# One order list for five engines: attention first, first-layer products in two large groups

## The chip, the cores and the metric

The kernel runs on one core of one Trainium2 chip. The metric is device microseconds (us) of one execution; lower is better. The engines are named as the profile names them: PE is TensorE's matrix multiplication and PEld its weight loads, DVE is VectorE, ACT is ScalarE, POOL is GpSimd, SP is SyncE, whose queue issues every DMA here.

## The reference

```
attn_out = attention(q, k, v)            # 2 batches x 12 heads, 448 tokens, head size 64, causal, float32
x = attn_out -> (896 tokens, 768)
h = x @ w_in                             # 768 -> 1024
solu = h * softmax(h);  ln = layernorm(solu) * g_ln
x = ln @ w_out                           # 1024 -> 768, the first block ends
h = max(x @ w_in2, 0);  out = (h * h) @ w_out2      # 768 -> 2048 -> 768, the second block
```

## The kernel before

Attention works on 12 pairs of heads (pair i of 0 to 11; pairs 0 to 5 are batch 0). Every float32 product after it is split: an operand is kept as a rounded part (hi) and a rest (lo), and three products replace one. The weights come as 64-bit floats, so DVE first puts a raw tile together with three integer operations (`as_f32`, lines 151 to 153).

Everything up to the second block is written as an order list, `SEQ`: names such as `Sa.7`, an operation and its index. A loop (line 732) hands the operations out in that order. Each engine runs its own operations in the order in which the list names them; between engines only data and buffers hold things back. So the list fixes five queues, and nothing else in the program depends on it. The names that matter here:

- SP: `load_r` (keys and queries of a pair into one of 4 `KQ` buffers, 448 KB), `load_v` (one of 3 `VR` buffers, 256 KB), `lq` (a quarter of a 1 MB weight tile of the first layer; `lq.8` to `lq.11` are tile 2), `ld` (a whole one, tiles 3 to 5), `rowd` (row maxima into `MR`, two small DMAs), `sums`, `rcd`, `spread` (denominators out, to DRAM, and back over all partitions), `lw` (weights of the second product), `load_g`.
- ACT: `H` (rounds `KQ`), `row`, `ea1` and `eb1` (exponentials of the scores), `E` (the unnormalised output out of PSUM), `x_hi`, `wh` (hi of a weight tile).
- DVE: `mxa`, `mxb`, `mxc` (row maxima), `recips`, `x_lo`, `wf` (`as_f32`), `wl` (lo of a weight tile), and `mx`, `mu` and others of the layernorm.
- POOL: `ka` and `kb` (causal mask), `ad` (adds for the row sums), `norm` (multiplies by the reciprocals, L421).
- PE: `fl` (filler products), `S0a`, `S0b`, `S0c` (rough scores for the maxima), `mT` (a transpose), `Sa` and `Sb` (scores), `Ua` and `Ub` (times v, L353), `Us` (row sums, L377), `h<t>.<c>` (first-layer products of token tile t with weight tile c, six matrix products, L497), `T` (transposes for the layernorm), `y0`, `y1` (second product).

PSUM is handed out in four slots of two banks. A slot is taken by `S0`, `S`, `U`, a token tile of `h`, `T` or `y`, and goes to the next taker in the order in which the list gives it back: by `mxa` and `mxb`, by `row`, by `ea1` and `eb1`, by `E`, and for an `h` tile by `sq`, its square in the layernorm:

```python
        def bank2(nm):
            pl = slots.pop(0)
...
            def h_part(b, t, c):
                for s, w in ((0, 0), (0, 1), (1, 0)):
                    for half in range(2):
                        nc.tensor.matmul(
                            b[:, half, :],
                            xT[c][s][:, t * P : t * P + P],
                            W1[c][:, w, 512 * half : 512 * half + 512],
```

So `h<t>.<c>` needs `x_hi` and `x_lo` of the head pairs of block c and of the batch of tile t, and `wh.<c>` and `wl.<c>`. Three token tiles (0 to 2) lie in batch 0 alone.

Of the kernel before, what the change touches and what calls it, by code (L numbers as in the profile page):

```python
# [27 lines left out]
SEQ = """
load_r.0 fl.0 fl.1 fl.2 H.0 fl.3 fl.4 S0c.0 fl.5 load_r.1 load_r.2 H.1 mxc.0 load_r.3 S0a.0 lq.0 fl.6 fl.7 S0b.0 S0a.1
fl.8 mxa.0 mxb.0 ld.3 S0b.1 mxr.0 H.2 mxa.1 mxb.1 Sa.0 load_v.0 S0c.1 H.3 S0b.2 S0b.3 mxc.1 ea1.0 mT.1 row.1 mxb.2  # L30
Sb.0 S0a.2 ka.0 lq.4 S0c.2 mxb.3 rowd.1 lq.1 eb1.0 mxa.2 load_r.4 lq.2 Sa.1 S0a.3 ea1.1 Ua.0 mxc.2 mT.2 kb.0 Sb.1
row.2 S0c.3 mxa.3 H.4 Ub.0 load_g.0 ad.0 eb1.1 mxc.3 ka.1 load_v.1 S0b.4 mT.3 rowd.2 Us.0 row.3 S0a.4 mxb.4 E.0
load_r.5 Sa.2 kb.1 S0c.4 Sb.2 mxa.4 lq.3 ea1.2 sums.0 load_v.2 mxc.4 eb1.2 Ua.1 rowd.3 ad.1 mT.4 recips.0 Sb.3 Ub.1
wf.0 Us.1 row.4 ka.2 H.5 lq.8 kb.2 eb1.3 rcd.0 S0a.5 Sa.3 E.1 load_r.6 ea1.3 ad.2 S0b.5 rowd.4 spread.0 ka.3 Sa.4
S0c.5 H.6 sums.1 mxa.5 mxb.5 lq.5 Sb.4 load_r.7 kb.3 S0a.6 recips.1 mxc.5 rcd.1 load_v.3 ea1.4 mT.5 norm.0 row.5 eb1.4
Ua.2 S0b.6 Ub.2 lq.6 H.7 S0c.6 mxa.6 mxb.6 spread.1 ka.4 Us.2 x_hi.0 rowd.5 Ua.3 S0a.7 mxc.6 E.2 ad.3 mT.6 lq.7 sums.2
x_lo.0 kb.4 load_r.8 S0b.7 load_v.4 wh.0 Ub.3 mxa.7 row.6 rowd.6 norm.1 Us.3 mxb.7 recips.2 S0c.7 Sb.5 E.3 x_hi.1 H.8
Sa.5 mxc.7 sums.3 mT.7 row.7 eb1.5 Sa.6 rcd.2 wf.1 recips.3 ad.4 ea1.5 x_lo.1 S0b.8 kb.5 ea1.6 load_r.9 spread.2 Sb.6
Ua.4 Ub.4 S0c.8 eb1.6 rowd.7 ka.5 mxb.8 H.9 norm.2 load_r.10 ad.5 S0a.8 mxa.8 rcd.3 Us.4 Sa.7 load_v.5 S0b.9 mxc.8 E.4
ea1.7 sums.4 Sb.7 mxb.9 S0a.9 mT.8 recips.4 kb.6 ka.7 Ua.5 spread.3 x_hi.2 row.8 S0c.9 Ub.5 H.10 load_r.11 rcd.4 mxa.9  # L40
mxc.9 x_lo.2 S0a.10 mT.9 eb1.7 rowd.8 ka.6 norm.3 Us.5 S0b.10 ad.6 row.9 lq.9 wh.1 mxa.10 Sa.8 Sb.8 load_v.6 E.5 H.11
mxb.10 rowd.9 load_v.7 S0c.10 wl.0 ea1.8 Ua.6 Ub.6 mxc.10 sums.5 kb.7 spread.4 S0b.11 x_hi.3 mT.10 recips.5 eb1.8
lq.10 row.10 Us.6 rcd.5 load_v.8 S0a.11 x_lo.3 norm.4 mxb.11 lq.11 rowd.10 Sa.9 ad.7 Ua.7 load_v.9 spread.5 mxa.11
wl.1 E.6 Ub.7 S0c.11 ka.8 Sb.9 ea1.9 mxc.11 x_hi.4 Sb.10 eb1.9 mT.11 Us.7 x_lo.4 h0.0 eb1.10 sums.6 wf.2 row.11 h1.0
norm.5 Sa.10 E.7 rowd.11 recips.6 wf.3 h1.1 ld.4 rcd.6 Ua.8 kb.8 ea1.10 Ub.8 ka.10 load_v.10 h0.1 wh.2 wl.2 h1.2 wh.3
Sb.11 ad.8 wl.3 h0.2 x_hi.5 h0.3 ld.5 load_v.11 spread.6 sums.7 h1.3 Us.8 eb1.11 x_lo.5 wf.4 norm.6 wh.4 E.8 ka.9 h2.0
recips.7 h2.2 wf.5 kb.9 h2.3 wl.4 Sa.11 rcd.7 wh.5 sums.8 x_hi.6 spread.7 recips.8 h2.1 wl.5 h0.4 lw.0 x_lo.6 h0.5
ea1.11 ad.9 Ua.9 Ub.9 rcd.8 mx.0 Us.9 norm.7 ka.11 h1.4 kb.10 of.0 E.9 h1.5 x_hi.7 mx.1 lw.1 ex.0 sums.9 ex.1 h2.4
Ua.10 h2.5 ad.10 Ub.10 recips.9 mu.0 mu.1 sq.0 h5.0 sq.1 Us.10 x_lo.7 spread.8 h5.1 de.1 norm.8 rcd.9 h3.0 x_hi.8 lw.2
kb.11 E.10 mx.2 x_lo.8 ex.2 Ua.11 ad.11 va.1 pw.1 h3.1 Ub.11 spread.9 de.0 norm.9 va.0 Us.11 sums.10 de.2 h5.2 oh.0  # L50
recips.10 x_hi.9 E.11 mu.2 rcd.10 pw.0 ol.0 fa.1 h4.0 sq.2 h4.2 spread.10 of.1 x_lo.9 sums.11 recips.11 va.2 ln.1
rcd.11 oh.1 fa.0 of.2 norm.10 spread.11 lw.3 h3.2 ln.0 h3.3 T.0 h5.3 x_hi.10 x_lo.10 h3.4 oh.2 pw.2 h4.3 ol.1 fa.2
h4.4 Th.0 Tl.0 T.1 ol.2 norm.11 x_hi.11 ln.2 x_lo.11 h3.5 Th.1 of.3 mx.3 h4.1 oh.3 h4.5 h5.4 Tl.1 T.2 ex.3 mu.3 de.3
h5.5 lw.4 sq.3 mx.4 h6.0 Th.2 va.3 pw.3 ex.4 mx.5 fa.3 h6.3 Tl.2 ln.3 mu.4 h6.1 T.3 ex.5 mu.5 de.4 Th.3 h6.4 sq.5 Tl.3
h6.2 sq.4 of.4 ol.3 lw.5 h6.5 oh.4 va.4 pw.4 mx.6 of.5 y0.0 ol.4 ex.6 de.5 mu.6 va.5 fa.4 oh.5 sq.6 de.6 y0.1 ln.4
lw.6 y0.2 va.6 pw.6 y0.3 l2.1 ol.5 pw.5 T.4 of.6 fa.5 oh.6 y0.4 Th.4 lw.7 fa.6 ln.5 y0.5 ln.6 ol.6 Tl.4 of.7 T.5 Th.5
oh.7 Tl.5 l2.0 l2.2 ol.7 y0.6 T.6 Th.6 Tl.6 f2.0 y0.7 y1.0 yo.0 y1.1 g2.0 yp.0 yo.2 o2.0 yo.1 f2.1 yp.1 g2.1 o2.1 y1.2
yp.2
"""


# [794 lines left out]
```

## Time and profile before

| what | value |
|---|---|
| median of 3 runs | 445.75 us (445.51 to 446.55) |
| the profiled execution | 445.59 us |
| its span, first to last instruction | 443.9 us |
| PE busy | 435.9 us (98%) |
| DVE busy | 268.6 us (61%) |
| ACT busy | 162.8 us (37%) |
| POOL busy | 151.9 us (34%) |
| second block starts | 209.30 us |

The span is 1.7 us shorter than the profiled execution's own time. Places in the text are microseconds from the start of the span. Busy time of PE counts a product until its last result is out, so it counts short waits between pipelined products too.

### The profile page before, as it was taken

The page shows a single profiled execution, that of the slowest core. Times are in us where ns is not written, and L with a number is a line of the kernel's source. Part 1 is how long each engine was busy: PE and PEld are TensorE (multiplying, and loading weights), DVE is VectorE, ACT ScalarE, POOL GpSimd, SP SyncE. Part 2 cuts the span into 40 slices and gives each one's busy share as a digit, 9 for nine tenths or more (in the row PEclk, how much of TensorE's full clock was granted, in tenths as well). Part 3 has the DMA queues.
Part 4 walks back from the last instruction along what each step waited for, and adds up shares of the span by engine and source line. Part 5 has one row for each costly group of instructions (what it writes and reads, how often), then busy time and mean ns, then how long its engine had stood idle before and what let it go on. Part 6 is the DMA issues. An engine that isn't in the chain of part 4 may idle for free.

```text
span 443.9 us, 6457 instructions
## 1 busy us (share of the span) xinstructions
PE 435.9 (98%) x2487; PEld 372.0 (84%) x2487; DVE 268.6 (61%) x511; ACT 162.8 (37%) x223; POOL 151.9 (34%) x145
## 2 busy tenths in 40 slices
...
GB/s 252 201 180 212 156 209 158 144 165 99 38 235 17 326 14 1 0 0 1 71 84 130 102 113 123 91 142 73 142 71 143 76 138 88 251 109 103 127 16 124
DMA packets 33000, 52.45 MB, mean 118 GB/s; under 512 B 5962, under 2 KB 24394, under 8 KB 32586
## 3 DMA queue, kind: packets, MB, share of 16 engines
...
## 4 chain that ended last, share of the span: by engine, by line
PE 92%; DMA 3%; POOL 2%; ACT 1%; SPq 0%; issue 0%; DVE 0%; POOLq 0%; ACTq 0%
PE h L780 26%; PE o L780 26%; PE h L497 14%; PE y L645 13%; PE s L309 4%; PE U L353 4%; DMA KQ<-in_kq_dram 2%; PE mxp L251 1%; PE T L623 1%; PE U L377 1%; DMA VR<-in_v_dram 1%; PE s L320 1%; PE s L328 1%; POOL x L421 1%; PE fill L526 0%; ACT HI L241 0%
## 5 line engine op out<-in xcount | busy, mean ns | idle before, releaser
L701 POOL TENSOR_TENSOR w<-wf,w 128x768 fp32r<-128x768 f32 x32 | 59.1, 1847 | 209.0 <-ACT w L698 209.0
L780 PE MATMUL h<-yT,w 128*128 128x480 f32 x576 | 115.4, 362 | 0.0
L780 PE MATMUL o<-g,w 128*128 128x480 f32 x576 | 115.4, 362 | 0.0
L780 PEld LDWEIGHTS h<-yT,w 128*128 128x128 f32 x576 | 107.9, 187 | 7.4
L780 PEld LDWEIGHTS o<-g,w 128*128 128x128 f32 x576 | 107.9, 187 | 7.3
L151 DVE TENSOR_SCALAR wf<-raw 128x768 int32<-128x768 int32 (+1 forms) x46 | 28.3, 616 | 79.3 <-DMA raw<-in_moe_w_out_dram 55.3
L698 ACT CAST w<-wf 128x768 fp32r<-128x768 f32 x32 | 26.8, 836 | 134.9 <-DVE wf L153 116.0
L497 PE MATMUL h<-w,xT 128*128 128x512 f32 x252 | 61.8, 397 | 0.0
L645 PE MATMUL y<-lnT,w 128*128 128x384 f32 (+1 forms) x288 | 59.1, 365 | 0.0
L645 PEld LDWEIGHTS y<-lnT,w 128*128 128x128 f32 x288 | 51.9, 188 | 6.1
L497 PEld LDWEIGHTS h<-w,xT 128*128 128x128 f32 x252 | 46.1, 188 | 11.1 <-issue 1.6
L152 DVE SCALAR_TENSOR_TENSOR wf<-raw,wf 128x768 int32<-128x768 int32 (+1 forms) x46 | 49.0, 1064 | 1.6
L153 DVE SCALAR_TENSOR_TENSOR wf<-raw,wf 128x768 int32<-128x768 int32 (+1 forms) x46 | 46.1, 1002 | 1.6
L266 DVE CUSTOM_DVE_ANT_0 JK<-mxp,MK 112x336 bf16<-112x336 f32 (+2 forms) x96 | 39.3, 446 | 10.6 <-PE mxp L251 9.3
L341 POOL TENSOR_SCALAR_AFFINE_SELECT PP<-PP 128x256 f32<-128x256 f32 (+1 forms) x48 | 26.4, 579 | 17.8 <-ACT PP L344 17.8
L344 ACT ACTIVATE PP<-s 128x1024 f32<-128x1024 f32 x24 | 24.2, 1018 | 17.1 <-PE s L320 14.7
L309 PE MATMUL s<-KQ 64*128 64x448 f32 (+3 forms) x192 | 26.6, 396 | 0.4 <-ACT PP L344 0.4
L762 DVE TENSOR_TENSOR relu<-h,relu 128x896 f32<-128x896 f32 x16 | 17.5, 1092 | 14.6 <-ACT relu L761 14.6
L353 PE MATMUL U<-PP,VR 128*64 128x448 f32 (+3 forms) x192 | 25.0, 389 | 0.9 <-DMA VR<-in_v_dram 0.7
L367 POOL TENSOR_TENSOR ps<-ps,PP 128x384 f32<-128x384 f32 (+1 forms) x24 | 24.7, 1030 | 1.9
L309 PEld LDWEIGHTS s<-KQ 64*128 64x128 f32 x192 | 16.7, 186 | 8.7 <-issue 5.3
L353 PEld LDWEIGHTS U<-PP,VR 128*64 128x64 f32 x192 | 11.6, 136 | 13.4 <-issue 9.0
...
## 6 DMA issues: line engine op xcount, KB each, us to landing
...
```

The source lines that it names most:

```text
L151: nc.vector.tensor_scalar(xi, hw, 3, 0x3FFFFFFF, ALU.logical_shift_left, ALU.bitwise_and)
L152: nc.vector.scalar_tensor_tensor(xi, hw, -0x40000000, xi, ALU.bitwise_and, ALU.bitwise_or)
L153: nc.vector.scalar_tensor_tensor(xi, lw, 29, xi, ALU.logical_shift_right, ALU.bitwise_or)
L266: nc.vector.tensor_tensor_reduce(JK[t], b[0:JP, h, o : o + nk], MK[:, S - nk :], 1.0, NEG, ALU.add, ALU.max, mx[i][:, 4 * h + t : 4 * h + ...
L309: nc.tensor.matmul(s[:, h, o : o + nq], K[r, P * t : P * t + P], Q[r, q0 : q0 + nq], start=t == HALF[a][0][0], stop=False,)
L341: nc.gpsimd.affine_select(ap, ap, [[0, 2], [1, m]], ALU.is_ge, 0.0, base=0, channel_multiplier=-1)
L353: nc.tensor.matmul(UB[i][D * h : D * h + D, 0, q0:S], VR[i % 3][:, t, h, :], PP[(2 * i + a) % NPP][:, h, o : o + nq], start=t == 0, stop=t ...
L497: nc.tensor.matmul(b[:, half, :], xT[c][s][:, t * P : t * P + P], W1[c][:, w, 512 * half : 512 * half + 512], start=(c == 0 and s == 0 and ...
L645: nc.tensor.matmul(b[:, ci, 0:n], WO[fi][:, w, c * P : c * P + P], M["lnT"][a][s][:, fi, :], start=(fi == 0 and w == 0 and s == 0), stop=( ...
L698: nc.scalar.copy(W2[n][:, 0], w_f["2", n])
L701: nc.gpsimd.tensor_tensor(W2[n][:, 1], w_f["2", n], f(W2[n][:, 0]), ALU.subtract)
L780: nc.tensor.matmul(flat(b)[:, o : o + n], w[:, wp, c : c + P], ops[s][:, x : x + n], start=first and r == 0, stop=last and r == 2,)
```

## The change

Only `SEQ` is replaced. It holds the same 585 operations, in another order; from `T.0` on the two lists differ little. The parts that matter, cut (a line of "..." is left-out text):

```diff
-Sb.0 S0a.2 ka.0 lq.4 S0c.2 mxb.3 rowd.1 lq.1 eb1.0 mxa.2 load_r.4 lq.2 Sa.1 S0a.3 ea1.1 Ua.0 mxc.2 mT.2 kb.0 Sb.1
-row.2 S0c.3 mxa.3 H.4 Ub.0 load_g.0 ad.0 eb1.1 mxc.3 ka.1 load_v.1 S0b.4 mT.3 rowd.2 Us.0 row.3 S0a.4 mxb.4 E.0
...
-x_lo.0 kb.4 load_r.8 S0b.7 load_v.4 wh.0 Ub.3 mxa.7 row.6 rowd.6 norm.1 Us.3 mxb.7 recips.2 S0c.7 Sb.5 E.3 x_hi.1 H.8
-Sa.5 mxc.7 sums.3 mT.7 row.7 eb1.5 Sa.6 rcd.2 wf.1 recips.3 ad.4 ea1.5 x_lo.1 S0b.8 kb.5 ea1.6 load_r.9 spread.2 Sb.6
-Ua.4 Ub.4 S0c.8 eb1.6 rowd.7 ka.5 mxb.8 H.9 norm.2 load_r.10 ad.5 S0a.8 mxa.8 rcd.3 Us.4 Sa.7 load_v.5 S0b.9 mxc.8 E.4
-ea1.7 sums.4 Sb.7 mxb.9 S0a.9 mT.8 recips.4 kb.6 ka.7 Ua.5 spread.3 x_hi.2 row.8 S0c.9 Ub.5 H.10 load_r.11 rcd.4 mxa.9
-mxc.9 x_lo.2 S0a.10 mT.9 eb1.7 rowd.8 ka.6 norm.3 Us.5 S0b.10 ad.6 row.9 lq.9 wh.1 mxa.10 Sa.8 Sb.8 load_v.6 E.5 H.11
...
-lq.10 row.10 Us.6 rcd.5 load_v.8 S0a.11 x_lo.3 norm.4 mxb.11 lq.11 rowd.10 Sa.9 ad.7 Ua.7 load_v.9 spread.5 mxa.11
-wl.1 E.6 Ub.7 S0c.11 ka.8 Sb.9 ea1.9 mxc.11 x_hi.4 Sb.10 eb1.9 mT.11 Us.7 x_lo.4 h0.0 eb1.10 sums.6 wf.2 row.11 h1.0
-norm.5 Sa.10 E.7 rowd.11 recips.6 wf.3 h1.1 ld.4 rcd.6 Ua.8 kb.8 ea1.10 Ub.8 ka.10 load_v.10 h0.1 wh.2 wl.2 h1.2 wh.3
-Sb.11 ad.8 wl.3 h0.2 x_hi.5 h0.3 ld.5 load_v.11 spread.6 sums.7 h1.3 Us.8 eb1.11 x_lo.5 wf.4 norm.6 wh.4 E.8 ka.9 h2.0
-recips.7 h2.2 wf.5 kb.9 h2.3 wl.4 Sa.11 rcd.7 wh.5 sums.8 x_hi.6 spread.7 recips.8 h2.1 wl.5 h0.4 lw.0 x_lo.6 h0.5
-ea1.11 ad.9 Ua.9 Ub.9 rcd.8 mx.0 Us.9 norm.7 ka.11 h1.4 kb.10 of.0 E.9 h1.5 x_hi.7 mx.1 lw.1 ex.0 sums.9 ex.1 h2.4
-Ua.10 h2.5 ad.10 Ub.10 recips.9 mu.0 mu.1 sq.0 h5.0 sq.1 Us.10 x_lo.7 spread.8 h5.1 de.1 norm.8 rcd.9 h3.0 x_hi.8 lw.2
-kb.11 E.10 mx.2 x_lo.8 ex.2 Ua.11 ad.11 va.1 pw.1 h3.1 Ub.11 spread.9 de.0 norm.9 va.0 Us.11 sums.10 de.2 h5.2 oh.0
...
+mxb.2 lq.1 rowd.1 mxa.2 S0c.2 ka.0 S0b.3 Sa.1 load_r.4 load_v.1 eb1.0 kb.0 mxc.2 ad.0 mT.2 mxb.3 ea1.1 ka.1 lq.2 Sb.1
+row.2 S0a.3 S0c.3 Ua.0 load_v.2 rowd.2 H.4 Ub.0 load_r.5 mxa.3 eb1.1 mxc.3 lq.3 S0c.4 kb.1 S0a.4 ad.1 mT.3 Us.0 row.3
...
+lq.6 load_r.8 mxa.7 kb.4 S0c.7 rowd.6 S0b.7 recips.2 Us.3 Sb.5 rcd.2 lq.7 norm.1 wh.0 mxc.7 E.3 mxb.7 sums.3 x_hi.1
+Ua.4 eb1.5 ad.4 H.8 Sa.5 lq.9 ea1.5 mT.7 x_lo.1 row.7 Sb.6 spread.2 S0b.8 eb1.6 kb.5 Sa.6 S0a.8 recips.3 ea1.6
+load_r.9 Ub.4 wf.1 mxb.8 Us.4 S0c.8 mxa.8 H.9 norm.2 E.4 rowd.7 ka.5 mxc.8 rcd.3 Sa.7 S0a.9 load_v.5 Sb.7 ea1.7 mT.8
+ad.5 S0b.9 mxa.9 S0c.9 load_r.10 x_hi.2 row.8 Ua.5 kb.6 spread.3 x_lo.2 mxb.9 ka.6 norm.3 Ub.5 sums.4 load_v.6 ad.6
+load_g.0 rowd.8 Us.5 ka.7 wh.1 mxc.9 recips.4 wl.1 Sa.8 H.10 eb1.7 S0a.10 E.5 mT.9 kb.7 load_v.7 Sb.8 ea1.8 S0b.10
...
+S0c.11 rowd.10 mxc.11 Sb.9 ld.4 mT.11 ea1.9 Sa.10 row.11 eb1.9 wl.0 x_hi.4 Sb.10 sums.6 x_lo.4 rowd.11 Us.7 lq.11
+load_v.9 ea1.10 spread.5 Ua.8 eb1.10 Ub.8 kb.9 norm.5 Sb.11 Sa.11 recips.6 Us.8 wf.2 eb1.11 lw.0 wf.3 ea1.11 wh.2 E.7
+h1.0 x_hi.5 ld.5 wl.2 wh.3 h1.1 wl.3 rcd.6 ka.9 spread.6 ka.10 x_lo.5 wf.4 kb.11 norm.6 h0.0 ka.11 wh.4 h0.1 h2.0 h1.2
+kb.10 sums.7 recips.7 wf.5 rcd.7 E.8 load_v.10 h2.1 sums.8 h2.2 lw.1 h1.3 wl.4 ad.9 h0.2 h2.3 Ua.9 wh.5 x_hi.6 Ub.9
+h0.3 wl.5 x_lo.6 recips.8 h0.4 spread.7 h0.5 h1.4 lw.2 h1.5 mx.0 mx.1 ex.0 Us.9 norm.7 E.9 rcd.8 mu.0 h2.4 h2.5 Ua.10
+ex.1 sq.0 load_v.11 sums.9 Ub.10 Ua.11 x_hi.7 Ub.11 ad.10 de.0 mu.1 va.0 ad.11 spread.8 recips.9 de.1 Us.10 x_lo.7
+sq.1 norm.8 va.1 E.10 mx.2 of.0 rcd.9 sums.10 ex.2 x_hi.8 recips.10 Us.11 x_lo.8 spread.9 pw.0 fa.0 h4.0 h5.0 mu.2
...
```

Between `Us.7` and `T.0`, PE's list before has 12 stretches of `h` operations, with attention between them; the new list has 4, two of them of 11 and of 8 operations.

## Rows read from the trace of the kernel before

**Rows 1.** The page: the span, and each engine's busy us (share) and instructions.
```profile
span 443.9 us, 6457 instructions
PE 435.9 (98%) x2487; PEld 372.0 (84%) x2487; DVE 268.6 (61%) x511; ACT 162.8 (37%) x223; POOL 151.9 (34%) x145
```

**Rows 2.** Busy time by stretch: length; PE, PEld, DVE, ACT, POOL; granted clock, DMA.
```profile
10.00:70.00 60.00, 57.77 (x546) 37.59 (x546) 50.05 (x196) 40.17 (x61) 48.56 (x64) 1.00 0.65 193
70.00:209.30 139.30, 139.30 (x760) 112.92 (x757) 98.90 (x154) 61.17 (x89) 46.02 (x42) 1.00 0.27 92
```

**Rows 3.** Timeline of PE: start, us, instructions, idle time before it in brackets.
```profile
21.82 0.47 PE L251 MATMUL mxp<-HI 64*128 64x336 f32 x4 [0.52 <-ACT HI L241]
...
46.54 1.13 PE L309 MATMUL s<-KQ 64*128 64x320 f32 x8 [0.44 <-ACT PP L344]
...
61.22 1.63 PE L353 MATMUL U<-PP,VR 128*64 128x448 f32 x12 [0.74 <-DMA VR<-in_v_dram]
```

**Rows 4.** The chain that ended last, in order of time: start, us, what.
```profile
15.38 5.37 DMA KQ<-in_kq_dram
...
50.81 1.13 PE s L309 x8
51.94 0.28 PE s L320 x2
...
56.83 4.25 DMA VR<-in_v_dram
...
70.30 0.19 PE mxp L278
...
71.00 2.95 PE h L497 x12
...
75.36 1.57 PE h L497 x6
...
83.06 4.31 PE h L497 x18
87.37 0.51 PE U L377 x10
...
97.89 1.88 PE U L353 x16
...
104.60 1.02 PE U L353 x8
...
117.40 7.04 PE h L497 x30
```

**Rows 5.** Timeline of SP, DMAs issued: `lq.1`, `sums.2`, `sums.4`, and `ld.4` behind `rowd.11`.
```profile
14.89 0.39 SPq L481 DMA_DIRECT2D raw<-in_moe_w_in_dram  x1
...
39.53 0.60 SPq L394 DMA_DIRECT2D sc<-es  x1
...
51.42 0.62 SPq L394 DMA_DIRECT2D sc<-es  x1
...
72.75 0.40 SPq L126 DMA_DIRECT2D raw<-in_moe_w_in_dram  x1
```

**Rows 6.** Timeline of ACT: the first part of `E.3`, and `H.8`.
```profile
41.48 0.45 ACT L386 ACTIVATE es<-U,SE 97x224 f32<-97x224 f32 x1 [1.60 <-issue]
...
44.48 0.94 ACT L241 CAST HI<-KQ 128x896 fp32r<-128x896 f32 x1 [1.51 <-DMA KQ<-in_kq_dram]
```

**Rows 7.** Timeline of DVE: `recips.2`, start of `wf.1`, end of `mxb.8`; `wf.2`, `wl.5`.
```profile
42.29 0.20 DVE L400 RECIPROCAL sr<-sc 112x8 f32<-112x8 f32 x1 [0.47 <-DMA sc<-es]
...
43.12 0.89 DVE L151 TENSOR_SCALAR wf<-raw 128x1024 int32<-128x1024 int32 x1
...
49.24 0.07 DVE L266 DVE_READ_ACCUMULATOR2_ANT mx<- 112x1 f32 x1
...
69.43 0.89 DVE L151 TENSOR_SCALAR wf<-raw 128x1024 int32<-128x1024 int32 x1
...
92.79 1.91 DVE L492 TENSOR_TENSOR w<-wf,w 128x1024 fp32r<-128x1024 f32 x1
```

More of the change, by code (lines that the diff above doesn't have):

```diff
@@ L28 @@
 SEQ = """
-load_r.0 fl.0 fl.1 fl.2 H.0 fl.3 fl.4 S0c.0 fl.5 load_r.1 load_r.2 H.1 mxc.0 load_r.3 S0a.0 lq.0 fl.6 fl.7 S0b.0 S0a.1
-fl.8 mxa.0 mxb.0 ld.3 S0b.1 mxr.0 H.2 mxa.1 mxb.1 Sa.0 load_v.0 S0c.1 H.3 S0b.2 S0b.3 mxc.1 ea1.0 mT.1 row.1 mxb.2
-Sb.0 S0a.2 ka.0 lq.4 S0c.2 mxb.3 rowd.1 lq.1 eb1.0 mxa.2 load_r.4 lq.2 Sa.1 S0a.3 ea1.1 Ua.0 mxc.2 mT.2 kb.0 Sb.1
-row.2 S0c.3 mxa.3 H.4 Ub.0 load_g.0 ad.0 eb1.1 mxc.3 ka.1 load_v.1 S0b.4 mT.3 rowd.2 Us.0 row.3 S0a.4 mxb.4 E.0
-load_r.5 Sa.2 kb.1 S0c.4 Sb.2 mxa.4 lq.3 ea1.2 sums.0 load_v.2 mxc.4 eb1.2 Ua.1 rowd.3 ad.1 mT.4 recips.0 Sb.3 Ub.1
@@ L34 @@
-wf.0 Us.1 row.4 ka.2 H.5 lq.8 kb.2 eb1.3 rcd.0 S0a.5 Sa.3 E.1 load_r.6 ea1.3 ad.2 S0b.5 rowd.4 spread.0 ka.3 Sa.4
-S0c.5 H.6 sums.1 mxa.5 mxb.5 lq.5 Sb.4 load_r.7 kb.3 S0a.6 recips.1 mxc.5 rcd.1 load_v.3 ea1.4 mT.5 norm.0 row.5 eb1.4
-Ua.2 S0b.6 Ub.2 lq.6 H.7 S0c.6 mxa.6 mxb.6 spread.1 ka.4 Us.2 x_hi.0 rowd.5 Ua.3 S0a.7 mxc.6 E.2 ad.3 mT.6 lq.7 sums.2
-x_lo.0 kb.4 load_r.8 S0b.7 load_v.4 wh.0 Ub.3 mxa.7 row.6 rowd.6 norm.1 Us.3 mxb.7 recips.2 S0c.7 Sb.5 E.3 x_hi.1 H.8
-Sa.5 mxc.7 sums.3 mT.7 row.7 eb1.5 Sa.6 rcd.2 wf.1 recips.3 ad.4 ea1.5 x_lo.1 S0b.8 kb.5 ea1.6 load_r.9 spread.2 Sb.6
@@ L39 @@
-Ua.4 Ub.4 S0c.8 eb1.6 rowd.7 ka.5 mxb.8 H.9 norm.2 load_r.10 ad.5 S0a.8 mxa.8 rcd.3 Us.4 Sa.7 load_v.5 S0b.9 mxc.8 E.4
-ea1.7 sums.4 Sb.7 mxb.9 S0a.9 mT.8 recips.4 kb.6 ka.7 Ua.5 spread.3 x_hi.2 row.8 S0c.9 Ub.5 H.10 load_r.11 rcd.4 mxa.9
-mxc.9 x_lo.2 S0a.10 mT.9 eb1.7 rowd.8 ka.6 norm.3 Us.5 S0b.10 ad.6 row.9 lq.9 wh.1 mxa.10 Sa.8 Sb.8 load_v.6 E.5 H.11
-mxb.10 rowd.9 load_v.7 S0c.10 wl.0 ea1.8 Ua.6 Ub.6 mxc.10 sums.5 kb.7 spread.4 S0b.11 x_hi.3 mT.10 recips.5 eb1.8
-lq.10 row.10 Us.6 rcd.5 load_v.8 S0a.11 x_lo.3 norm.4 mxb.11 lq.11 rowd.10 Sa.9 ad.7 Ua.7 load_v.9 spread.5 mxa.11
```

24 lines of the change are left out of this document (16 added, 8 removed).

## The prediction

> **What bounds the kernel now.** I read the page first, then busy time by stretch, then PE's own timeline for its idle time, then the chain that ended last, and last the queues of SP, ACT and DVE at the few places that the new order touches. PE is busy 435.9 of 443.9 us [rows 1]; the change moves none of its 2487 products to another engine and takes none away, so it can gain or lose only in the gaps between them. From 70 to 209.30 us PE has no idle time at all, and from 10 to 70 it has 60.00 − 57.77 = 2.23 us [rows 2]. The granted clock is 1.00 in both stretches, the upper level (2.4 GHz), so there is nothing to be had from it. Three idle places of PE in the attention stretch add up to 0.52 + 0.44 + 0.74 = 1.70 us [rows 3]. What follows 209.30 us is the second block, whose operations are not in the list; it moves as a whole.
>
> So the sum has three kinds of terms: products that cost less because of their neighbours, the three old waits, and new waits.
>
> **Fewer stretches of h (−1.7).** The chain gives four lengths of a stretch of h operations: one takes 1.57 us, two 2.95, three 4.31, five 7.04 [rows 4]. That is a line: 1.365 us for each operation and 0.21 for each stretch (1.365 + 0.21 = 1.575; 5 × 1.365 + 0.21 = 7.04). The list before has 12 stretches between Us.7 and T.0, the new one 4. 8 × 0.21 = 1.7 us less. The bounds are 0 and 1.7, and I take the whole, since the four rows agree to 0.01.
>
> A rule of the skill speaks against this term. The Trainium skill, TensorE: Matmul & The Clock Gate, Back-to-back issue gap, gives an isolated spacing of N ÷ 2.4 plus 2.5 ns for a product of N columns, the drain of one hidden behind the next; worked out from it, six products of 512 columns are an estimated 1.29 us wherever they stand, and a stretch costs nothing extra. By it this term and the next would be 0. The rows of one, two, three and five show otherwise, so I keep 0.21.
>
> **U operations side by side (−0.5).** An Ua or Ub alone takes 1.02 us, a pair that follows each other 1.88 [rows 4], so 2 × 1.02 − 1.88 = 0.16 less. I count five adjacent pairs in the list before and ten in the new one, and Ub.10 there also meets Ua.11: six new joints, 6 × 0.16 = 0.96 at most. What used to stand between them makes joints elsewhere, which no row prices; I take the middle of 0 and 0.96.
>
> **The three old waits (−1.7).** (a) S0b.4 waited 0.52 us for H.4, and H.4 for load_r.4, issued at 15.38 behind lq.1 (14.89) and landed 5.37 later [rows 3 to 5]. In the new list load_r.4 follows rowd.1 directly and lq.1 has been gone long before; issued at 14.89 even the same 5.37 us end at 20.26, and with an H of 0.94 us [rows 6] PE, which reached this point at 21.82 − 0.52 = 21.30, finds it done. (b) Sb.6 waited 0.44 for the PSUM slot of eb1.5, which on ACT stood behind H.8, and H.8 had kept ACT idle 1.51 us for its load [rows 3, 6]. In the new list eb1.5 stands ahead of H.8. (c) Ua.6 waited 0.74 for load_v.6, issued at 56.83 and 4.25 us on its way [rows 3, 4], behind rowd.8, lq.9 and a load_r. In the new list load_v.6 follows sums.4, which is issued at 51.42 [rows 5]: some five us earlier. All three go. (At the ends, pipelined products hide 0.1 or 0.2 us more of each wait; 2.1 is the other end.)
>
> **New wait 1: Sa.7 (+0.3).** Sa.7 takes its PSUM slot from mxb.8, in both lists; PE got there at 50.81 [rows 4]. DVE had it done at 49.31 [rows 7]. In the new list recips.3 stands ahead of wf.1, so DVE must first wait for sums.3 to land. sums.3 can leave when the first part of E.3 is written: 41.48 + 0.45 = 41.93 [rows 6], less a lead of some 0.8 by then (0.52 and three joints), 41.1. A transfer of that kind was awaited from 39.53 to 42.29, 2.76 us [rows 5, 7]; so recips.3 runs at 43.9, and wf.1 begins there instead of at 43.12. From wf.1's start to mxb.8's end is 49.31 − 43.12 = 6.19 us [rows 7], less for recips.3 and x_lo.1, which now stand ahead: mxb.8 ends at 49.3 to 50.1. PE comes at 50.81 − 0.52 − 0.44 − 0.25 = 49.6, earlier if more than the idle time is saved. Between 0 and 1.1; I take 0.3.
>
> **New wait 2: the weights of the first large group (+1.0).** In the list before 14 h operations stand ahead of Ua.9, in 6 stretches, and Ua.9 starts at 97.89 [rows 4]; in the new one 11 in one stretch, and otherwise the same. PE gets there at 97.89 − 3 × 1.365 − 5 × 0.21 − 1.7 − 0.4 + 0.3 = 91.0, and to h0.4, which needs wl.4, after 1.88 for Ua.9 and Ub.9 and 1.4 for h0.3: at 94.3; to h0.5, which needs wl.5, at 95.7. DVE's row from the start of wf.2 to the end of wl.5 was 94.70 − 69.43 = 25.3 us [rows 7]. wf.2 needs lq.11, and in the new list lq.11 stands on SP behind rowd.11, which waits for row.11 and that for mT.11. The group starts at 91.0 − 11 × 1.365 − 0.21 = 75.8; between mT.11 and it stand four S operations of 1.13 + 0.28 at most, a pair of U of 1.88 and two Us of 0.51 [rows 4], 8.5 us, so mT.11 ends at 67.3. Before, it ended at 70.49, and the DMA behind rowd.11 was issued at 72.75 [rows 4, 5], 2.26 later; here 69.6. A quarter tile then takes between 2.76 us (the tiny transfer above) and 4.25 (load_v.6, of the same size, with 700 KB ahead); I take 3.0, so wf.2 starts at 72.6, not at 69.43, and wl.5 would end at 97.9: 2.2 us late. Against that, POOL had two row adds (ad.8, ad.9) beside this row of DVE before and has one (ad.9) now. I bound the wait by 0 and 2.2 and take the middle, 1.0. Behind DVE, wh.4 and then E.8 on ACT wait for wf.4, and Ua.9 takes its PSUM slot from E.8; that is the same delay seen earlier, not a second one.
>
> The other moves I cost at nothing. load_g, ld.5 and the lw loads change places on SP; DVE's row on wf.2 to wf.4 covers ld.5 (a landing later than wf.4's end would delay wl.5 by as much), the layernorm of the first tiles covers lw.0. Us.9 to Us.11 need ad.9 to ad.11, now late on POOL behind norm.6 and norm.7, with about 6 us to spare; without it each would cost PE its lateness in full. Slots for Ua.10, Ua.11 and h4.0 come from E.9, sq.0 and sq.1, each more than 1 us before PE.
>
> **The sum.** −1.7 − 0.5 − 1.7 + 0.3 + 1.0 = −2.6. From the profiled execution's 445.59 that is 443.0; its median stands 0.16 higher, so 443.1.
>
> **The rivals.**
> 1. *The group starves.* For: lq.11 is behind a wait on SP, and DVE takes its operations in order. If lq.11 needs 4.25 us and DVE's row stretches by 3 us because POOL now has kb.9, ka.9, ka.10, kb.11, norm.5 and norm.6 at the same time, wl.5 ends at 69.6 + 4.25 + 28.3 = 102.2, 6.5 us late: 443.0 − 1.0 + 6.5 = 448.5. It decides against the change once wl.5 ends later than about 100. Against: POOL's adds are fewer there. A sentence of the Trainium skill bears on it, SBUF — State Buffer, Who interferes with whom: a DVE operation with two SBUF inputs and a POOL operation that reads SBUF block each other for a whole instruction. No run here shows that alone.
> 2. *New waits eat the gain.* PE was 98% busy; with both new waits at their bounds, 1.1 and 2.2, and the joints at 0, the sum is −1.7 − 1.7 + 3.3 = −0.1: 445.5. The case that a stretch costs nothing gives nearly the same, 443.0 + 1.7 + 0.5 = 445.2; the rows of four lengths leave it 0.03.
> 3. *No new wait.* If DVE is not held by POOL, wl.5 is in time: −1.7 − 0.96 − 2.1 = −4.8, so 440.8 at the utmost.
>
> **How the numbers follow.** The forecast with its own spread (441.5 to 444.7) has 0.56, rival 3 0.15, rival 2 0.17 (the 0.03 within it), rival 1 0.12. The likeliest is 443.1. The range leaves out the utmost of rival 3 and the larger part of rival 1: 441.2 to 445.9. Within 0.2% (0.9 us, about what a measurement of this kernel can tell) is 444.9 to 446.6: faster 0.71, same 0.17, slower 0.12.
>
> **What would show it.** Right: no idle time of PE before S0b.4, Sb.6 and Ua.6; stretches of 11 h operations in about 15.2 us; an idle place before Sa.7 of some tenths; wf.2 of DVE idle before its start, released by the raw load; PE idle before Ua.9 or h0.4, under 2.2 us in all; the second block starting near 206.7. Wrong: waits of PE on MR, which I take as landed everywhere; H.9 to H.11 late because their loads stand behind rcd and spread on SP; waits in the layernorm after T.0, where I found none but margins of a few tenths.

## The result and the profile after

The new list takes 442.22 us in the median (440.71 to 445.63, 18 runs), the one before beside it 445.88; the ratio is 0.9911 (95% interval 0.9882 to 0.994). Run again unchanged, it took 441.88 us, 0.9901 (0.9879 to 0.9924). The profiled execution took 442.1 us, 3.5 less than that of before; 443.1 was forecast, and 443.0 for the profiled execution.

The page and busy time by stretch, as in [rows 1, 2]:

```profile
span 440.3 us, 6462 instructions
PE 433.4 (98%) x2487; PEld 372.4 (85%) x2487; DVE 264.6 (60%) x511; ACT 163.2 (37%) x223; POOL 151.0 (34%) x145
...
10.00:70.00 60.00, 59.17 (x561) 38.13 (x557) 48.08 (x195) 41.22 (x62) 49.20 (x66) 1.00 0.63 197
70.00:205.34 135.34, 135.34 (x751) 112.75 (x748) 97.21 (x155) 60.68 (x87) 44.39 (x40) 1.00 0.28 92
```

PE is idle for 0.83 us from 10 to 70 (2.23 before) and never after that; the second block starts at 205.34, 3.96 sooner. The chain that ended last shows where that was won:

```profile
70.49 0.51 PE U L377 x10
71.00 1.89 PE U L353 x16
...
75.93 15.19 PE h L497 x66
91.13 1.88 PE U L353 x16
93.01 7.03 PE h L497 x30
...
100.55 2.96 PE h L497 x12
103.51 3.62 PE U L353 x32
107.12 0.89 PE U L377 x20
108.01 11.11 PE h L497 x48
```

The first line is Us.7. It ends at 71.00, and at 71.00 it ended before too [rows 4]; but the new order has then also done Sa.10, which before stood behind the first two h operations and took the 75.36 − 71.00 − 2.95 = 1.4 us between the two stretches there [rows 4]. So the attention side was worth 1.4 us in this execution. From the start of Us.7 to the second block the new list takes 205.34 − 70.49 = 134.85 us; before, 209.30 − 70.49 = 138.81 us (Us.7 takes 0.51), of which 1.4 is Sa.10. So the group side was worth 138.81 − 1.4 − 134.85 = 2.56 us. Added up from the two chains by kind of operation, each from the end of the one before it: the 42 h operations took 59.99 us before and 58.19 now, the 8 U operations 7.83 and 7.38; Sb.11 and Sa.11 took 1.30 and 1.40 apart and take 2.53 side by side; Us.10 and Us.11 took 1.03 and take 0.89.

The waits, in PE's timeline: S0c.4 and S0b.4, Sb.6, Ua.6 (no bracket: no idle time), and the one place that is new, Sb.7:

```profile
21.53 0.94 PE L251 MATMUL mxp<-HI 64*128 64x224 f32 x4
...
24.42 0.37 PE L251 MATMUL mxp<-HI 64*128 64x336 f32 x4
...
45.04 1.13 PE L309 MATMUL s<-KQ 64*128 64x320 f32 x8
...
52.02 1.14 PE L309 MATMUL s<-KQ 64*128 64x320 f32 x8 [0.29 <-ACT E L387]
...
59.97 1.95 PE L353 MATMUL U<-PP,VR 128*64 128x448 f32 x16
```

The three places of [rows 3] are gone. The rest of the 0.83 us is 0.43 at mT.1 (0.36 before), 0.10 at S0a.4 and parts of hundredths. DVE shows both new waits of the forecast: `recips.3` and `wf.1`, the last piece of `mxb.8`, and the row from `wf.2` to `wl.4` and `wl.5` (one line) [rows 7]:

```profile
44.95 0.20 DVE L400 RECIPROCAL sr<-sc 112x8 f32<-112x8 f32 x1 [1.55 <-DMA sc<-es]
45.15 0.90 DVE L151 TENSOR_SCALAR wf<-raw 128x1024 int32<-128x1024 int32 x1
...
49.73 0.08 DVE L266 DVE_READ_ACCUMULATOR2_ANT mx<- 112x1 f32 x1
...
72.92 0.69 DVE L151 TENSOR_SCALAR wf<-raw 128x1024 int32<-128x1024 int32 x1 [2.20 <-DMA raw<-in_moe_w_in_dram]
...
91.10 3.92 DVE L492 TENSOR_TENSOR w<-wf,w 128x1024 fp32r<-128x1024 f32 x2
```

`wf.2` started at 72.92 (forecast 72.6), but wl.5 ended at 91.10 + 3.92 = 95.02, not at 97.9. PE reached h0.5 at 95.80: nothing waited, with 0.78 us to spare.

### The profile page after: what moved, and what is told of

Read it like the earlier page. It is cut to its first block, busy times and chain, and to the rows that moved or that the text cites. A ratio compares the mean times of both kernels' runs of the same rounds, so it can differ in the third digit from the quotient of the medians.

```text
span 440.3 us, 6462 instructions
## 1 busy us (share of the span) xinstructions
PE 433.4 (98%) x2487; PEld 372.4 (85%) x2487; DVE 264.6 (60%) x511; ACT 163.2 (37%) x223; POOL 151.0 (34%) x145
## 4 chain that ended last, share of the span: by engine, by line
PE 87%; DVE 0%; ACT 0%; issue 0%
PE h L780 26%; PE o L780 26%; PE h L497 13%; PE y L645 13%; PE U L353 3%; PE s L309 2%; PE T L623 1%; PE U L377 1%; PE s L320 1%; PE mxp L251 0%; PE mxp L278 0%; DVE o L814 0%; ACT o L814 0%
## 5 line engine op out<-in xcount | busy, mean ns | idle before, releaser
L701 POOL TENSOR_TENSOR w<-wf,w 128x768 fp32r<-128x768 f32 x32 | 59.2, 1850 | 205.8 <-ACT w L698 205.8
L497 PE MATMUL h<-w,xT 128*128 128x512 f32 x252 | 59.4, 393 | 0.0
L153 DVE SCALAR_TENSOR_TENSOR wf<-raw,wf 128x768 int32<-128x768 int32 (+1 forms) x46 | 46.8, 1017 | 1.6
L152 DVE SCALAR_TENSOR_TENSOR wf<-raw,wf 128x768 int32<-128x768 int32 (+1 forms) x46 | 46.7, 1016 | 1.6
L341 POOL TENSOR_SCALAR_AFFINE_SELECT PP<-PP 128x256 f32<-128x256 f32 (+1 forms) x48 | 28.1, 617 | 14.2 <-ACT PP L344 14.1
L353 PE MATMUL U<-PP,VR 128*64 128x448 f32 (+3 forms) x192 | 23.6, 387 | 0.0
L674 DVE TENSOR_TENSOR yT<-y,yT 128x384 fp32r<-128x384 f32 (+1 forms) x12 | 7.3, 623 | 24.6 <-ACT yT L673 24.6
L421 POOL TENSOR_TENSOR x<-E,bc 128x448 f32<-128x448 f32 x12 | 15.9, 1327 | 17.8 <-DMA bc<-d 8.9
```

The costliest lines, as they stand in the source:

```text
L152: nc.vector.scalar_tensor_tensor(xi, hw, -0x40000000, xi, ALU.bitwise_and, ALU.bitwise_or)
L153: nc.vector.scalar_tensor_tensor(xi, lw, 29, xi, ALU.logical_shift_right, ALU.bitwise_or)
L341: nc.gpsimd.affine_select(ap, ap, [[0, 2], [1, m]], ALU.is_ge, 0.0, base=0, channel_multiplier=-1)
L353: nc.tensor.matmul(UB[i][D * h : D * h + D, 0, q0:S], VR[i % 3][:, t, h, :], PP[(2 * i + a) % NPP][:, h, o : o + nq], start=t == 0, stop=t ...
L497: nc.tensor.matmul(b[:, half, :], xT[c][s][:, t * P : t * P + P], W1[c][:, w, 512 * half : 512 * half + 512], start=(c == 0 and s == 0 and ...
L701: nc.gpsimd.tensor_tensor(W2[n][:, 1], w_f["2", n], f(W2[n][:, 0]), ALU.subtract)
```

## The experiments

Every list but the first changes a few places of the new list or joins the two. From the start of Us.7 to the second block the new list takes 134.85 us in the first trace and again in same_list, early_lq11 and undo_waits, so that stretch is compared from single traces. The attention side is not so steady: from the start of S0b.1 to the start of Us.7 it takes 60.2 to 62.3 us in ten traces of the new order (undo_waits left out) and 64.8 in pool_extra. What a list is worth there can't be read from one trace to better than a microsecond. In four kernels (same_list, early_lq11, late_lq11, split) the line numbers in the profile are lower by one.

**same_list.** The new list unchanged.

> The new list unchanged, as the measure for the other lists and to see what its runs differ in (the 18 runs of it so far lie between 440.71 and 445.63 us, those of the list before mostly between 445.2 and 446.7). Theory (every wait of PE in the large group is gone): median 442.2, second block from 205.3 in the trace, no idle place of PE after 70 us. Rival (PE waits for the weights of the group in some executions): a second trace may show the second block later, with idle time of PE ahead of h1.2, h0.4 or h0.5.

Measured: 441.88 us (441.01 to 442.34), ratio 0.9901. Us.7 starts at 69.53, Us.7 to the second block 134.85; no idle time behind 70 us. wl.5 ended at 92.88 this time, 2.0 us ahead of h0.5. So the theory holds for this trace, and the spare time differs from execution to execution.

**early_lq11 and late_lq11.** What is the late `lq.11` worth, and where does it begin to cost?

```diff
 early_lq11
-S0c.11 rowd.10 mxc.11 ... rowd.11 Us.7 lq.11 load_v.9
+S0c.11 lq.11 rowd.10 mxc.11 ... rowd.11 Us.7 load_v.9
 late_lq11
-rowd.11 Us.7 lq.11 load_v.9 ... spread.5 ... Us.8 wf.2 eb1.11 lw.0 wf.3
+rowd.11 Us.7 load_v.9 ... spread.5 ... Us.8 lw.0 lq.11 wf.2 eb1.11 wf.3
```

> New list with lq.11 alone moved: ahead of rowd.10, where the list before has it. Theory (the late lq.11 costs nothing, since wl.5 ends 0.8 us before h0.5): wf.2 starts about 2 us earlier (70.8, behind recips.6), second block from 205.3, median 442.2, the same as the list unchanged. Rival (lq.11 costs PE time in those executions that take over 443): median 0.5 to 1.0 lower and no run over 443. Second rival (wf.2 then meets ad.8 on POOL and DVE's row takes the 25.3 us that it took before): wl.5 ends near 96, second block up to 0.3 later.

> New list with lq.11 moved behind spread.5 and lw.0 on SP: issued at 72.3 in place of 69.5, and behind the bytes of lw.0. Theory (the group has 0.8 us to spare at h0.5, 1.3 at h1.2, 1.4 at Ua.9): wf.2 starts 3 to 5 us later, wl.5 ends at 98 to 100, and PE waits for it that much less 0.8: 2.2 to 4.2 us, second block from 207.5 to 209.5, time 444.4 to 446.4. Rival (DVE's row shortens by as much, since POOL is then less busy beside it): wl.5 under 97, second block from 205.3 to 206.3, time at most 443.2.

Measured: early_lq11 441.72 us, 0.9909 (0.9881 to 0.9937). wf.2 starts at 71.00 with no wait, wl.5 ends at 93.41, Us.7 to the second block 134.85: the same as unchanged. One run of it took 444.37, so not all of the longer runs come from the late lq.11; the first rival is not borne out, and the second is out (the row took 22.4 us).

late_lq11 444.87 us, 0.9995 (0.9969 to 1.0021): no gain that the runs can tell. In its trace the second block starts at 207.73, so 2.4 of the 3.96 us are gone and not all. The chain that ended last now runs through the load, DVE's row and h0.5; below it, PE's idle places, in its timeline:

```profile
71.95 5.30 DMA raw<-in_moe_w_in_dram
...
77.28 0.70 DVE wf L150
...
96.38 2.04 DVE w L491
...
98.46 3.96 PE h L496 x16
```
```profile
82.39 2.11 PE L496 MATMUL h<-w,xT 128*128 128x512 f32 x8 [0.92 <-ACT E L386]
84.81 8.00 PE L496 MATMUL h<-w,xT 128*128 128x512 f32 x34 [0.31 <-DVE w L491]
98.46 1.90 PE L496 MATMUL h<-w,xT 128*128 128x512 f32 x7 [0.31 <-DVE w L491]
```

wf.2 starts 4.4 us later than in the first trace and wl.5 ends at 98.42, 3.4 later. From Us.7 to the second block it takes 137.37 us, 2.5 more; 3.4 less the 0.8 to spare is 2.6. The brackets add to 1.54; the rest must lie between pipelined products, where the profile counts PE as busy. One path was not in the theory: E.7 stands behind wh.2 on ACT, and h2.0 takes its slot from E.7 (the 0.92). This is rival 1 of the prediction made to happen: the group starves, by 2.5 us, when its last weight comes 3.4 later.

**split.** Does a stretch cost anything?

```diff
-Ua.8 eb1.10 Ub.8 kb.9 norm.5 Sb.11 Sa.11 recips.6 Us.8 ... h1.0 ... h1.1 ... h0.0 ... h2.3 Ua.9 ... Ub.9 h0.3
+eb1.10 kb.9 norm.5 Sb.11 Sa.11 recips.6 ... h1.0 Ua.8 ... h1.1 Ub.8 ... h0.0 Us.8 ... h2.3 Ua.9 ... h0.3 Ub.9
```

> New list with Ua.8, Ub.8 and Us.8 moved into the first large group (behind h1.0, h1.1 and h0.0) and Ub.9 behind h0.3: four more stretches of h operations, two pairs of U operations taken apart, the same products. Theory (0.21 us for each stretch, 0.16 for each pair): 4 x 0.21 + 2 x 0.16 = 1.2 us, second block from 206.5, time 443.4. Rival (a stretch costs nothing, as the spacing rule has it): second block from 205.3, time 442.2. Each stretch can be read in the trace as well: one h operation alone 1.57 us by the theory, 1.37 by the rival.

In this list the exponentials of pair 11 take the place of those of pair 8 before Ua.8 and Ub.8 read them, so pair 8 of the output is another; the products are the same in number and size. Measured: 442.85 us, 0.9921 (0.9899 to 0.9944). The chain that ended last:

```profile
73.14 1.58 PE h L496 x6
74.73 1.02 PE U L352 x8
75.75 1.59 PE h L496 x6
77.33 1.01 PE U L352 x8
78.35 1.58 PE h L496 x6
...
80.44 11.12 PE h L496 x48
```

One h operation alone takes 1.58 to 1.59 us, a U alone 1.01 or 1.02. From the start of Us.7 (70.10) to the second block (206.18) it takes 136.08 us, 1.23 more than unchanged, where 1.16 was worked out. The rival (0) is out. The Trainium skill, TensorE: Matmul & The Clock Gate, Back-to-back issue gap, gives an isolated spacing by a product's own columns alone; at these joints the measured time is longer, and depends on the neighbours.

**attn_only, attn_slot and group_only.** What is each half worth alone? The halves meet at Us.7; in all three lq.11 stands as before.

```diff
 attn_only: the new order up to Us.7, from there the order before
 group_only: the order before up to Us.7, from there the new order
 attn_slot (against attn_only):
-E.7 recips.6 wf.3 h1.1 rcd.6 Ua.8 ea1.10 Ub.8
+recips.6 wf.3 h1.1 rcd.6 ea1.10 Ua.8 E.7 Ub.8
```

> The new order up to Us.7, from there the order before; lq.11 stands where the list before has it, so that the weights don't come late. Theory (from the first trace after: at Us.7 PE is 1.3 us ahead, the old waits less what the start-up took; the rest of the gain is made behind it): second block near 207.9, time 444.4. Rival A (the old waits and their removal are the whole gain): second block near 205.5, time 442.2. Rival B (the waits come back elsewhere before the second block): 209.3, 445.6.

> The order before up to Us.7, from there the new order with its two large groups. Theory (8 stretches fewer at 0.21, and U operations side by side, 2.5 us in the first trace after): second block near 206.8, time 443.2. Rival A (a stretch costs nothing): second block at 209.0, time 445.4. Rival B (the group waits for its weights when attention ahead of it ends as late as before): PE idle before h0.4 or h0.5, second block over 207.5.

> The list of attn_only with E.7 moved behind ea1.10 and Ua.8, so that Ua.8 takes its PSUM slot from ea1.10; in attn_only it took the slot of E.7, which waited for norm.5, and PE stood 1.02 us. Theory (the attention part alone is worth 1.3 us, less what that wait took): no idle time before Ua.8, and from the start of S0b.1 to the second block 198.4 to 198.8 us (200.1 in the trace before, 199.5 in attn_only, 195.8 in the first trace after); time 444.3. Rival (the attention part is worth nothing by itself): 199.5 to 200.1, time 445.3 or more.

Measured: group_only 443.8 us, 0.9954 (0.9931 to 0.9977); attn_only 445.34, 1.0007 (0.9989 to 1.0026); attn_slot 446.19, 0.9989 (0.9955 to 1.0023). In group_only, Us.7 to the second block takes 136.25 us, of which 1.4 is Sa.10: the new list's 134.85. Its second block starts at 207.93 where 206.8 was expected, because the start-up took 2.2 us longer in that execution (last section) and attention 1.0 less; PE waits for no weights. So the group half is worth what the trace said.

The attention half alone is worth too little for the runs to tell, and here the theory failed, twice. In the trace of attn_only, which starts S0b.1 at 9.08 as the list before does, the second block starts at 208.71, 0.59 us sooner than before: a lead of 1.6 at Us.7 (1.4 of it is Sa.10, done ahead) less the wait of 1.02 shown first here. PE's idle places behind Us.7, attn_only first, then attn_slot:

```profile
76.13 1.09 PE L353 MATMUL U<-PP,VR 128*64 128x448 f32 x8 [1.02 <-ACT E L387]
```
```profile
81.89 1.19 PE L497 MATMUL h<-w,xT 128*128 128x512 f32 x4 [1.39 <-DVE w L492]
```

When attention ends sooner, the old order behind it waits: Ua.8 for the slot of E.7, and with that slot exchanged h1.2 for wl.2. In attn_slot PE also waited in attention itself (1.00 us at S0c.4 and S0a.4, 0.36 at Sa.7, 0.29 at Sb.7), and Us.7 began 1.5 us later than in attn_only, with the same order up to there; from S0b.1 to the second block it took 201.1 us, more than either expectation. In the new list a pair of U, two S and a Us more stand between Us.7 and the first h operation, and in none of its traces does PE wait there.

**undo_waits.** Did the three places make the old waits?

```diff
-Sa.1 load_r.4 load_v.1 eb1.0
+Sa.1 load_v.1 load_r.4 eb1.0
-Ua.4 eb1.5 ad.4 H.8 Sa.5
+Ua.4 H.8 eb1.5 ad.4 Sa.5
-sums.4 load_v.6 ad.6 load_g.0 rowd.8 ... load_v.7 ... load_r.11
+sums.4 ad.6 load_g.0 rowd.8 ... load_v.7 ... load_r.11 load_v.6
```

> New list with three things undone: load_r.4 behind load_v.1, H.8 ahead of eb1.5 on ACT, load_v.6 behind load_v.7 and load_r.11. Theory (these three places made the old waits): PE idle again, before S0c.4, Sb.6 and Ua.6, some 0.5 us at each and 1.2 to 2.5 in all, and the second block as much later: 205.8 to 207.2, time 443.2 to 444.6. Rival (idle time there is taken out of waits that come later anyway, mT and Sb.7): second block under 205.5, time 442.0.

Measured: 444.59 us, 0.9971 (0.9945 to 0.9996). PE's timeline:

```profile
22.74 0.47 PE L251 MATMUL mxp<-HI 64*128 64x448 f32 x2 [0.55 <-ACT PP L344]
...
46.11 0.81 PE L309 MATMUL s<-KQ 64*128 64x320 f32 x4 [0.23 <-ACT PP L344]
...
62.61 1.63 PE L353 MATMUL U<-PP,VR 128*64 128x448 f32 x12 [1.99 <-DMA VR<-in_v_dram]
```

PE waits at the three places again, 2.8 us in all, a little more than was expected; Us.7 starts at 73.13, 2.6 later than in the first trace, and from there it takes 134.85 us as in the list unchanged. So the second block starts at 207.98, behind the 205.8 to 207.2 that were expected. The first wait came by another path: H.4, late, holds up eb1.1 behind it on ACT, and S0a.4 takes that slot. load_v.6 was put further back than it had stood, so 1.99 is more than the 0.74 of [rows 3]. The rival is out: nothing behind takes these waits in.

**pool_ad8, pool_extra and pool_extra_b.** Why was DVE's row shorter than 25.3 us?

```diff
 pool_ad8
-Sa.9 ad.8 S0c.11 ... recips.6 Us.8 wf.2 ... wl.3 rcd.6 ka.9 spread.6 ... h1.2 kb.10
+Sa.9 S0c.11 ... recips.6 wf.2 ... wl.3 rcd.6 ad.8 ka.9 spread.6 ... h1.2 Us.8 kb.10
 pool_extra, pool_extra_b
-wl.3 rcd.6 ka.9 spread.6
+wl.3 rcd.6 ad.8 ka.9 spread.6      (ad.8 a second time)
```

> New list with ad.8 moved on POOL behind norm.5, beside DVE's work on the weights of the first large group, and Us.8 behind h1.2 (it needs ad.8); ad.8 then adds the exponentials of pair 11, so the row sums of pair 8 are others. DVE took 25.3 us from wf.2 to wl.5 in the trace before, 22.1 and 21.0 in the two traces of the new list. Theory (DVE's row was shorter than forecast because POOL had one row add less beside it): 23.5 to 26 us, wl.5 ends at 96 to 98, PE waits 0.5 to 2 us before h0.4 or h0.5, time 442.8 to 444.2 (0.2 of it for one stretch more). Rival (POOL's other work beside DVE, ka, kb and norm, costs as much as an add): 21 to 22.5 us, no wait, time 442.1.

> New list with one operation more: ad.8 a second time on POOL behind norm.5, beside DVE's work on the weights; nothing reads its sum. In the four traces of the new order DVE took 19.6 us from the start of wf.2 to the end of wl.4, and 20.5 to 22.4 to the end of wl.5. Theory (a row add of POOL beside DVE's operations lengthens them): 21 to 23 us to the end of wl.4, 22.5 to 25 to the end of wl.5, PE idle before h0.4 or h0.5 by 0.5 to 2 us, and perhaps before Us.9 too, since ad.9 then ends 3 us later than before (it had 3.3 to spare); time 442.4 to 444.5. Rival (only the bytes of SBUF that DVE moves count, POOL's work does not): 19.6 us to the end of wl.4, no wait before h0.4 and h0.5.

> The list of pool_extra once more (ad.8 a second time behind norm.5), for a second profile: in its first one the start-up took 2 us longer than in the others. There DVE took 21.4 us from wf.2 to the end of wl.4 (19.2 to 20.9 in the traces of the new order), PE waited 1.16 us at Ua.9 for E.8's slot, and not at h0.4 or h0.5. Theory (a row add beside DVE makes wf.3 and wl.2 longer, and the delay reaches PE by way of wf.4, wh.4 and E.8): 20.5 to 22 us, PE idle 0.5 to 1.5 us before Ua.9, from the start of S0b.1 to the second block 196.2 to 197.3. Rival (the longer row was an accident of that execution): 19.2 to 20, no idle time there, 195.2 to 195.9.

pool_ad8 took 455.68 us (1.0215), and its time says nothing on the question: Us.8 also reads a buffer of exponentials that pair 11 had by then been given, and PE waited 10.92 us at it, for ka.11 on POOL; behind that wait the granted clock was 0.50 (1.2 GHz) from 88 to 101 us. pool_extra took 445.63 us, 0.9984 (0.9955 to 1.0013), pool_extra_b 446.14, 0.9975 (0.9941 to 1.0008). In both, from wf.2 to the end of wl.4 DVE took longer, 21.4 and 21.3 us; unchanged, it takes 19.6 and 19.7, and at most 20.9 in any other list that follows the new order there (undo_waits, where wl.4 met ad.9). The medians lie above what was expected. Both traces have a start-up longer by 2 us (last section), and both lose more in attention than the first trace, so from S0b.1 to the second block pool_extra_b takes 198.5 us, not the 196.2 to 197.3 expected; what the rest of the medians is made of is not shown. The lowest runs are 442.69 and 442.58. The trace of pool_extra is of its longest run (449.43): Sa.7 waited 2.06 us for mxb.8 there, and the granted clock fell to 0.5 (1.2 GHz) at 54.68, for 3.4 us. The line below is Sa.7, whose eight products took 1.19 us in the first trace:

```profile
54.71 2.19 PE L309 MATMUL s<-KQ 64*128 64x448 f32 x8 [2.06 <-DVE mx L266]
```

Only DVE's row is read from it. POOL, DVE, ACT and PE in pool_extra_b, around the added ad.8 (80.96 to 86.87):

```profile
80.96 2.55 POOL L365 TENSOR_TENSOR ps<-PP,PP 128x640 f32<-128x640 f32 x1
83.59 3.28 POOL L367 TENSOR_TENSOR ps<-ps,PP 128x384 f32<-128x384 f32 x2
...
93.04 2.10 POOL L421 TENSOR_TENSOR x<-E,bc 128x448 f32<-128x448 f32 x1
...
99.77 1.57 POOL L365 TENSOR_TENSOR ps<-PP,PP 128x640 f32<-128x640 f32 x1
```
```profile
80.02 2.06 DVE L152 SCALAR_TENSOR_TENSOR wf<-raw,wf 128x1024 int32<-128x1024 int32 x1
82.12 2.47 DVE L153 SCALAR_TENSOR_TENSOR wf<-raw,wf 128x1024 int32<-128x1024 int32 x1
...
89.42 1.23 DVE L152 SCALAR_TENSOR_TENSOR wf<-raw,wf 128x1024 int32<-128x1024 int32 x1
```
```profile
95.17 0.53 ACT L387 COPY E<-U 128x448 f32<-128x448 f32 x1 [1.76 <-POOL x L421]
```
```profile
95.76 1.63 PE L353 MATMUL U<-PP,VR 128*64 128x448 f32 x12 [1.11 <-ACT E L387]
```

Beside the added ad.8 the two steps of wf.3 take 2.06 and 2.47 us instead of 1.23, and ad.8's own first step 2.55 instead of the 1.57 of ad.9, which here ran beside little. So a row add beside DVE does lengthen its row, by up to 1.7 us. PE's wait at Ua.9 was forecast for pool_extra_b, but came by another way: POOL's norm.6 was late behind the add, E.8's second half waited for it, and Ua.9 for E.8's slot. wl.5 itself was still 1.7 us ahead of h0.5. From Us.7 to the second block: 136.2 us, 1.4 more.

**longer_group.** Can the lesson be used further?

```diff
+lq.11 ahead of rowd.10
-h2.3 Ua.9 wh.5 x_hi.6 Ub.9 h0.3 ... h0.4 spread.7 h0.5 h1.4 lw.2 h1.5 mx.0
+h2.3 wh.5 x_hi.6 h0.3 ... h0.4 spread.7 h1.4 h0.5 lw.2 h1.5 Ua.9 Ub.9 mx.0
```

> New list with lq.11 ahead of rowd.10 and the first large group made longer: h1.4 ahead of h0.5, and Ua.9 and Ub.9 moved behind h1.5, next to Us.9, so that 16 h operations stand in one stretch. Theory (0.21 us a stretch; with lq.11 early the weights come 1.5 us before they are wanted): one stretch less, 0.2 us off the time from S0b.1 to the second block, 195.0 to 195.7 us there, median 441.6, which the runs can't tell from the list unchanged. Rival (wl.4 and wl.5, wanted 1.9 us sooner, are late): PE idle before h0.4 or h0.5, time above 442.2.

Measured: 441.49 us (440.5 to 441.84), 0.991 (0.9891 to 0.993). The chain:

```profile
69.16 0.51 PE U L377 x10
...
74.60 21.99 PE h L497 x96
...
203.78 6.25 PE h L780 x31
```

16 h operations take 21.99 us (16 × 1.365 + 0.21 = 22.05), no weight is late, and from Us.7 to the second block it takes 134.62 us, 0.23 less. From S0b.1 it takes 194.7 us, under the 195.0 to 195.7 expected, since its attention side was the shortest of all traces of the new order. It is the fastest list here, by less than the runs can tell from the new one.

## Why the prediction was right, and where it was not

The forecast's side and size hold: −2.6 us was summed, −3.5 came in the profiled execution. The difference is in the joints and in new wait 2.

- **Fewer stretches (−1.7): right.** 15.19, 11.11, 7.03 and 2.96 us for stretches of 11, 8, 5 and 2 against 15.23, 11.13, 7.04 and 2.94 by 1.365 an operation and 0.21 a stretch; split shows the 0.21 by experiment.
- **U side by side (−0.5): the mechanism right, mis-sized.** Only three of the six new joints lie behind Us.7; there the U operations take 0.45 us less (3 × 0.16 = 0.48), four in a row 3.62 (4 × 1.02 = 4.08). The other three lie in attention, where the U operations took 16.02 us before and 15.36 now, added up in the same way, 0.6 to 0.7 less (the end of an old wait is in the 16.02). So the term was worth about 1.1, at the upper bound of 0.96 or over it, and not the middle. The joints elsewhere, which no row priced, gained as well: 0.17 where Sb.11 meets Sa.11 and 0.14 where Us.10 meets Us.11.
- **Three old waits (−1.7): the mechanism right, the size that of one execution.** All gone in the first trace, and waits at the three places again when undone. But group_only, the other trace of the old attention order, has only Sb.6's 0.44 of the three, and 0.39 at S0b.8; S0b.4 and Ua.6, which wait for loads, don't wait there, where PE comes 2 us later. Two details were wrong. load_v.6 was issued at 52.77, four us earlier than before and not five. load_r.4 was issued at 15.50, not at 14.89, because rowd.1 waited for row.1; its load took less long, and H.4 was still done (21.03) before S0c.4 (21.53). Those 0.5 us do not always suffice: in attn_slot, with the same order, H.4 started 0.9 later, at 20.99, and PE waited 0.44 at S0c.4 and 0.56 at S0a.4.
- **New wait 1 (+0.3): the size came right by luck, the path was another.** In the first trace Sa.7 did not wait: mxb.8 ended at 49.81, as reckoned (49.3 to 50.1), and PE came at 49.87. Instead Sb.7 lost 0.29 to E.4, behind H.9 on ACT, whose load stood behind spread.2 on SP; the prediction named that path only as a way to be wrong. In later traces of the same order Sa.7 did wait for mxb.8: 0.14 us in pool_extra_b, 0.36 in attn_slot, 1.23 in pool_ad8 and 2.06 in pool_extra, nearly twice the upper bound of 1.1; in the other eight of twelve it did not. So the forecast path exists, but its size was not bounded.
- **New wait 2 (+1.0): this step failed.** Its first half came out closely (group start 75.8 forecast and 75.93 measured, wf.2 72.6 and 72.92, Ua.9 91.0 and 91.13), in part by luck: a longer start-up (0.54) and more gain in attention (0.63) nearly cancel there. What failed is "the middle" between 0 and 2.2: DVE's row was carried over from before as 25.3 us, and took 22.1 (21.0 in same_list). ad.8 ran from 67.62 to 72.01, before wf.2 began, where in the old order it ran beside the row (77.56 to 82.84); pool_extra and pool_extra_b show that one add beside it is worth up to 1.7 us. The two timelines of DVE agree: from wl.2 to the end of x_lo.5, beside ad.8, the order before took 77.39 to 82.45, the new one 80.23 to 83.54, 1.75 less. Of the rest of the 3.2, 0.32 was a wait for wh.2 inside the old row, 0.2 were recips.6 and recips.8, which now stand outside it, and 0.6 lie in wl.4 and wl.5 (90.16 to 94.70 before, 91.10 to 95.02 now); why those two took longer is not shown. late_lq11 shows that the limit itself was placed rightly.

```profile
77.39 3.78 DVE L492 TENSOR_TENSOR w<-wf,w 128x1024 fp32r<-128x1024 f32 x2 [0.32 <-ACT w L488]
```

So the second block came at 205.34 and not at 206.7, 1.36 us sooner: 1.0 for wait 2, and 0.99 because the joints gave more than the 0.5 summed (0.86 on the group side; 0.63 on the attention side beyond the idle time that the timeline names, by the sums above nearly all in its U operations), less 0.09 for new waits in attention and 0.54 for a start-up that was longer in this execution (mT.1 at 13.54, 13.00 before). Of the 3.96 us by which the second block came sooner, the execution kept 3.5: from there to the end of the span it took 235.0 us, 234.6 before. The prediction let this part move as a whole; 234.57 us in the three traces with the old order behind T.0 (the list before, attn_only, attn_slot) and 234.7 to 235.1 in the others say that it does not quite. Why is not shown.

What the prediction did not see is that the attention half needs the other. It added their terms; group_only (−0.46%) and attn_only (+0.07%) together fall short of the −0.9 to −1.0% of the whole list, by a little more than their intervals. The trace of attn_only says why: the old order behind Us.7 turns 1.02 us of the lead into a wait.
